# Two attention blocks on one core: V in loads of two octets, fewer remainder transposes by DMA, the first x in three parts, output in place

## The chip, the cores and the metric

The kernel runs on one core of a Trainium2 chip. The metric is the device time of one execution in microseconds; a time is the median of several runs, and one further execution was taken with the hardware profiler. [...]

## The reference

Two problems, A and B, with the same shapes and data of their own; their results stand side by side in the output.

```python
# per problem: x 16x80x576, k_cache and v_cache 16x16x512x128, wq 576x4096, wo 4096x576, all bf16
q = (x @ wq).reshape(B, Sq, 32, 128).transpose(0, 2, 1, 3)
k = jnp.repeat(k_cache, 2, axis=1)      # 16 KV heads serve 32 query heads
v = jnp.repeat(v_cache, 2, axis=1)
scores = jnp.einsum("bhqd,bhkd->bhqk", q, k) * (128 ** -0.5)
p = softmax(scores)
o = jnp.einsum("bhqk,bhkd->bhqd", p, v)
out = o.transpose(0, 2, 1, 3).reshape(B, Sq, 4096) @ wo
```

## The kernel before

**Steps.** An octet is four KV heads with their eight query heads. A step U takes one octet of one batch row; there are 128 steps, 64 for each problem. Octets go in pairs: an even step and the odd step after it take two neighbouring octets of the same batch row in turn, for the eight batch rows of one half of the batch. Each KV head of a step has two query heads of 80 rows, 160 rows. The first 128 of them make one tile of scores (512 keys wide); the last 32 of all four heads are packed into a fifth tile, the remainder. So a step has five tiles of 128x512: `qk` (L678) for four of them and `qkr` (L665) for the remainder.

**Path of a tile.** Scores in PSUM; the maximum on DVE (`em_max`, L687); the exponential on ACT with its row sum (`em_exp`, L691), which writes a slot of `p_sb`; the reciprocal on DVE (L697); the scaling on POOL (`em_nrm`, L700). TensorE then transposes P in 64x64 pieces (`em_tr`, L733), and DVE or ACT evicts it into `pT`: two evictions for the four main tiles (`ptev`, L751 and L752), two for the remainder (`prev`, L757 and L758). With `rtr` true the remainder of a step isn't transposed on TensorE: a DMA transpose (L740) on SP's queue takes it from `p_sb` into `pT`, and neither its eight transposes nor its two evictions are there. That holds for odd steps from `RT0` to `RT1`. `pv` (L781) multiplies with V, `oev` (L795) evicts to `oT`.

**Around the steps.** `qp` (L542) and its tail `qt` (L555) project x for later steps, `qev` (L568, L569) evicts Q. `op` (L827) multiplies a finished half of the heads with Wo in 20 pieces of 128x288 for each half of the heads. The first half's result goes into `acc` (L839, fp32); the second half's is added to it on DVE (`em_eb`, L856), written as bf16 into one of two buffers `osb` and stored (`em_st`, L862).

**Loads.** All go through SP's queue. K comes transposed by DMA, 1 MB for two steps, into one of three pairs of buffers (`em_ldk`, L631). V comes as 512 KB for each step into one of six buffers (`em_ldv`, L635). x of problem A comes in two parts for each half of the batch (L380); it lies in the memory of `acc`, which is free until the first output. TensorE transposes it (`xtr`, L401, and `xt`, L419). Wq comes in four pieces for the first two octets (L507, and L511 for its last 64 rows).

**Order.** Every operation belongs to a stream with a letter. The string `ORDER`, written out by hand, names the streams one after another; each letter takes the next operation of that stream, a quote mark puts it on the other of DVE and ACT, and digits give the PSUM banks. Each engine runs its operations in that order. `finalize` works out from reads and writes what an operation waits for; an engine that waits holds up everything behind it in its own order. Before the first transposes TensorE runs `NWARM` matmuls on zeros (L353).

## Time and profile before

| | us |
|---|---|
| median of 3 runs | 720.44 |
| lowest and highest | 718.01, 720.6 |
| profiled execution | 720.92 |
| its span, first to last instruction | 719.0 |

The granted TensorE clock was 1.0 in the profiled execution. Busy times are sums over instructions. The chain that ended last is followed back from the last instruction, at each step to what released it. "PE" is the matmuls, "PEld" the weight loads, which run beside them; "SPq" is SP's queue, and its entries are the issuing of DMAs. In the waits, a row names who waited, for whom, the microseconds in total, how many times, and the longest.

### The profile page before, as it was taken

To read this page: it belongs to the slowest core of one execution; us is meant where nothing else is said; L and a number is where in the kernel's file an instruction comes from. 1 tells how busy PE (TensorE), PEld (TensorE's weight loads), DVE (VectorE), ACT (ScalarE), POOL (GpSimd) and SP (SyncE) were. 2 spreads that over 40 slices of the span, in tenths; PEclk is the share of its full clock that TensorE was granted. 3 is DMA by queue.
4 is the path that set the end of the run, shared out by engine and by line. 5 is a ranking of instruction groups with operands and counts; after the bars stand their busy time and mean duration, and the time that the engine had idled before them with its cause. 6 is when DMAs were issued, how large, how long until landed. Compare 5 with 4: busy or idle time off the path is not lost.

```text
span 719.0 us, 25863 instructions
## 1 busy us (share of the span) xinstructions
PE 712.0 (99%) x10604; PEld 508.8 (71%) x10604; DVE 630.0 (88%) x1419; ACT 637.5 (89%) x1830; POOL 431.9 (60%) x650
## 2 busy tenths in 40 slices
PE   9999999999999999999999999999999999999998
PEld 5576777777777777777777776767677777777777
DVE  3999998899978998899998899878898889998995
ACT  1999998899988998799988999888999898998994
POOL 0467657566655765755774566645676466665783
PEclk9999999999999999999999999999999999999999
DMA  9999999999799998999999999999999999999970
GB/s 238 275 217 240 273 252 250 286 232 244 175 268 241 220 241 194 258 223 240 255 216 248 226 201 206 228 246 239 220 229 204 279 196 261 225 247 221 211 195 18
DMA packets 388853, 164.23 MB, mean 228 GB/s; under 512 B 293248, under 2 KB 385664, under 8 KB 388736
## 3 DMA queue, kind: packets, MB, share of 16 engines
q1 hardware_dynamic: 388736, 162.59, 100.2%
q8 instruction: 84, 1.38, 0.8%
q14 instruction: 33, 0.27, 0.2%
HBM read 87.65 MB, written 2.95 MB: 126 GB/s over the span
## 4 chain that ended last, share of the span: by engine, by line
PE 93%; DMA 2%; DVE 2%; ACT 1%; SPq 0%; issue 0%; ACTq 0%; DVEq 0%
PE ps L827 22%; PE ps L781 20%; PE ps L542 18%; PE ps L678 15%; PE ps L733 10%; PE ps L665 5%; PE ps L555 4%; DVE negmax L687 2%; DMA pT<-p_sb 1%; DMA wq_sb<-in_A_wq_dram 1%; DMA out_dram<-osb 1%; ACT p_sb L691 0%; ACT qT L568 0%; DVE xT L406 0%; DVE qT L569 0%
## 5 line engine op out<-in xcount | busy, mean ns | idle before, releaser
L700 POOL TENSOR_SCALAR p_sb<-p_sb,rinv 128x512 bf16<-128x512 bf16 x640 | 430.1, 692 | 271.4 <-DVE rinv L697 270.8
L691 ACT ACTIVATE p_sb<-ps,negmax 128x512 bf16<-128x512 f32 x640 | 442.7, 713 | 27.3 <-DVE negmax L687 23.5
L687 DVE TENSOR_REDUCE negmax<-ps 128x1 f32<-128x512 f32 x640 | 419.2, 682 | 35.0 <-PE ps L678 30.3
L781 PE MATMUL ps<-pT,v_sb 128*128 128x160 bf16 x2048 | 191.2, 233 | 1.1 <-ACT p_sb L691 0.8
L781 PEld LDWEIGHTS ps<-pT,v_sb 128*128 128x128 bf16 x2048 | 152.8, 98 | 42.6 <-ACT p_sb L691 4.1
L827 PE MATMUL ps<-wo_sb,oT 128*128 128x288 bf16 x1280 | 181.1, 286 | 0.0
L678 PE MATMUL ps<-kT,qT 128*128 128x512 bf16 x512 | 178.0, 380 | 1.2 <-ACT p_sb L691 0.8
L542 PE MATMUL ps<-xT,wq_sb 128*128 128x320 bf16 x1024 | 174.4, 299 | 0.2 <-DMA wq_sb<-in_A_wq_dram 0.2
L827 PEld LDWEIGHTS ps<-wo_sb,oT 128*128 128x128 bf16 x1280 | 122.0, 98 | 42.5 <-ACT p_sb L691 0.8
L691 ACT ACTIVATION_READ_ACCUMULATOR p_sb<-ps,negmax 128x1 f32 x640 | 146.0, 228 | 0.0
L542 PEld LDWEIGHTS ps<-xT,wq_sb 128*128 128x128 bf16 x1024 | 95.4, 98 | 45.0 <-ACT p_sb L691 2.4
L751 ACT COPY pT<-ps 128x512 f32<-128x512 f32 x157 | 92.4, 602 | 13.3 <-PE ps L733 12.8
L733 PEld LDWEIGHTS ps<-ident,p_sb 64*128 64x128 bf16 x4904 | 88.2, 95 | 7.3 <-issue 1.3
L733 PE MATMUL ps<-ident,p_sb 64*128 64x64 bf16 x4904 | 92.4, 190 | 0.3 <-issue 0.2
L752 DVE COPY pT<-ps 128x1024 bf16<-128x1024 bf16 x99 | 67.3, 684 | 11.4 <-PE ps L733 10.0
L568 ACT ACTIVATE qT<-ps 128x320 bf16<-128x320 f32 x133 | 59.0, 458 | 19.3 <-PE ps L555 15.5
L569 DVE TENSOR_SCALAR qT<-ps 128x320 bf16<-128x320 f32 x123 | 58.2, 482 | 10.7 <-PE ps L555 6.1
L795 DVE CAST oT<-ps 128x320 bf16<-128x320 f32 x122 | 58.4, 482 | 7.7 <-PE ps L781 7.4
L678 PEld LDWEIGHTS ps<-kT,qT 128*128 128x128 bf16 x512 | 48.0, 97 | 24.1 <-ACT p_sb L691 4.1
L795 ACT CAST oT<-ps 128x320 bf16<-128x320 f32 x134 | 58.9, 451 | 5.2 <-PE ps L781 4.9
L697 DVE RECIPROCAL rinv<-rowsum 128x3 f32<-128x3 f32 (+1 forms) x256 | 38.4, 160 | 1.8 <-ACT p_sb L691 1.7
L665 PE MATMUL ps<-kT,qT 128*32 128x512 bf16 x512 | 39.2, 384 | 0.0
(31 smaller groups left out, 175.5 us busy)
## 6 DMA issues: line engine op xcount, KB each, us to landing
v_sb<-in_A_v_cache_dram SPq DMA_DIRECT2D x64, 512.0 KB, 5.0
v_sb<-in_B_v_cache_dram SPq DMA_DIRECT2D x64, 512.0 KB, 5.2
wo_sb<-in_A_wo_dram SPq DMA_DIRECT2D x8, 576.0 KB, 5.8
wo_sb<-in_B_wo_dram SPq DMA_DIRECT2D x8, 576.0 KB, 5.8
wq_sb<-in_B_wq_dram SPq DMA_DIRECT2D x4, 1024.0 KB, 6.9
out_dram<-osb SPq DMA_DIRECT2D x40, 72.0 KB, 3.8
wq_sb<-in_A_wq_dram SPq DMA_DIRECT2D x8, 256.0 KB, 4.7
wq_sb<-in_A_wq_dram SPq DMA_DIRECT2D x2, 1024.0 KB, 8.4
```

The costliest lines, as they stand in the source:

```text
L542: last = e.matmul(ps[:, vbq[h].phys, QO:QO + 320], lhsT=wq_sb[:, wsl, ck, hi * 128:(hi + 1) * 128], rhs=xT[:, half, ck, n0:n0 + 320], star ...
L665: last = e.matmul(ps[32 * g4:32 * g4 + 32, vb_.phys, :], lhsT=qT[:, qsl_, bl_, g4 * 160 + 128:g4 * 160 + 160], rhs=k_of(U_, g4), start=Tru ...
L678: return e.matmul(ps[:, vb.phys, :], lhsT=qT[:, qsl, bl, gl * 160:gl * 160 + 128], rhs=k_of(U, gl), start=True, stop=True)
L687: return e.tensor_reduce(negmax[:, si:si + 1], ps[:, vb.phys, :], axis=AX.X, op=AluOpType.max, negate=True)
L691: return e.activation(p_sb[:, psl, :], ps[:, vb.phys, :], AF.Exp, bias=negmax[:, si:si + 1], scale=1.0, accum_out=rowsum[:, ss, k:k + 1])
L700: return e.tensor_scalar(p_sb[:, psl, :], p_sb[:, psl, :], rinv[:, ss, k:k + 1], 1.0, op0=AluOpType.mult, op1=AluOpType.mult)
L733: last = e.matmul(dst, lhsT=p_sb[64 * h:64 * h + 64, psls[k_], j * 128:(j + 1) * 128], rhs=ident[64 * h:64 * h + 64, 64 * h:64 * h + 64], ...
L751: return e.copy(dst.bitcast(F32), ps[:, vtp[h].phys, :].rearrange("p (j n) -> p j n", j=4))
L752: return e.tensor_copy(dst, psb[:, vtp[h].phys, :].rearrange("p (j n) -> p j n", j=4))
L781: last = e.matmul(ps[:, vo.phys, off:off + 160], lhsT=v_sb[:, vs, gl, j * 128:(j + 1) * 128], rhs=pT[:, pts, j, :, 32 * gl:32 * gl + 32], ...
L795: return (e.copy if en == "act" else e.tensor_copy)(dst, src)
L827: last = e.matmul(ps[:, vb.phys, 0:DC], lhsT=oT[:, sp_ * (HH // 2) + i, rb * 128:(rb + 1) * 128], rhs=wo_sb[:, 2 * c3 + sp_, i, :], start= ...
```

## The change

Four things, and an `ORDER` that is written anew throughout.

- **V** is loaded at even steps only, by one DMA of 1 MB for the step's own octet and the next one's, into a pair of neighbouring buffers; the load waits for both buffers. 64 loads instead of 128.
- **Remainder of P.** `RT0` goes from 71 to 97: the odd steps 71 to 95, thirteen of them, transpose their remainder on TensorE again and evict it; the odd steps 97 to 123, fourteen, keep the DMA.
- **First x.** x of the first half of the batch comes in three parts of one, two and two blocks of 128 rows instead of three and two. The one block is issued from ACT's queue, the others from SP's. `NWARM` goes from 8 to 5.
- **Output in place.** The last addition writes bf16 over the first half of the fp32 values that it reads in `acc`, and the store reads it there. `osb` is gone; an addition no longer waits for an earlier store.

On SP's queue the beginning changes from x (3 blocks), Wq 0, x (2 blocks), two of Wq's last rows, Wq 1, Wq 2 to x (2 blocks), Wq 0, two of Wq's last rows, x (2 blocks), Wq 1, Wq 2.

```diff
-NWARM = 8
+NWARM = 5
+VM = 1
...
-RT0 = 71
+RT0 = 97
...
-XLD = ((-100.0, -85.0), (-5.0, -4.9))
+XLD = ((-100.0, -99.9, -85.0), (-5.0, -4.9))
+XENG = (("act", "sp", "sp"), ("sp", "sp"))
...
-        XP = ((0, 3), (3, 5))
+        XPS = (((0, 1), (1, 3), (3, 5)), ((0, 3), (3, 5)))
...
-                S.add("sp", XLD[half][part], em_ldx,
+                S.add(XENG[half][part], XLD[half][part], em_ldx,
...
-            def em_ldv(e, vc_ap=vc_ap, b=b, q=q, vs=vs):
-                src = vc_ap[b, 4 * q:4 * q + 4, :, :].rearrange("g (p j) d -> p g (j d)", j=4)
-                return e.dma_start(v_sb[:, vs, :, :], src)
+            vw = 2 if VM else 1
+
+            def em_ldv(e, vc_ap=vc_ap, b=b, q=q, vs=vs, vw=vw):
+                src = vc_ap[b, 4 * q:4 * q + 4 * vw, :, :].rearrange("(w g) (p j) d -> p w g (j d)", w=vw, j=4)
+                return e.dma_start(v_sb[:, vs:vs + vw, :, :], src)
...
-            S.add("sp", 5.0 * U - VK, em_ldv, writes=[R(("V", vs), U)],
-                  dsem="d_v%d" % vs, name="ldv%d" % U, stream="V")
+            if U % vw == 0:
+                S.add("sp", 5.0 * U - VK, em_ldv, writes=[R(("V", (U + i_) % NV), U + i_) for i_ in range(vw)],
+                      dsem="d_v%d" % vs, name="ldv%d" % U, stream="V")
...
-                                return e.tensor_tensor(osb[:, slot, :], ps[:, vb.phys, 0:DC],
+                                return e.tensor_tensor(xs[:, rb, 2 * c3 * DC:(2 * c3 + 1) * DC], ps[:, vb.phys, 0:DC],
                                                        acc[:, rb, c3 * DC:(c3 + 1) * DC], AluOpType.add)
...
-                                return e.dma_start(dst, osb[:, slot, :])
+                                return e.dma_start(dst, xs[:, rb, 2 * c3 * DC:(2 * c3 + 1) * DC])
...
-                                  writes=[R(("osb", slot), (prob, half, n))], name="oeb%d.%d.%d" % (prob, half, n),
+                                  writes=[R(("acc", rb, c3), (prob, hh))], name="oeb%d.%d.%d" % (prob, half, n),
```

`xs` is the same memory as `acc`, read as bf16.

## The prediction

> **What bounds the kernel now.** I read the page of the profile first, then the busy time by stretches, then the chain in order of time, then the waits of single engines.

> ```profile
> span 719.0 us, 25863 instructions
> PE 712.0 (99%) x10604; PEld 508.8 (71%) x10604; DVE 630.0 (88%) x1419; ACT 637.5 (89%) x1830; POOL 431.9 (60%) x650
> ...
> PE 93%; DMA 2%; DVE 2%; ACT 1%; SPq 0%; issue 0%; ACTq 0%; DVEq 0%
> ```

> TensorE is busy 99% of the span and is 93% of the chain that ended last. A busy share alone could be an average over unlike stages, so the stretches come next (columns: length, then busy time and count of PE, PEld, DVE, ACT, POOL, then clock, DMA share, GB/s).

> ```profile
> 320.00:360.00 40.00, 40.00 (x649) 28.69 (x647) 39.52 (x93) 39.65 (x119) 26.58 (x41) 1.00 1.10 240
> ...
> 400.00:440.00 40.00, 39.84 (x580) 28.38 (x578) 36.32 (x82) 37.73 (x107) 26.04 (x39) 1.00 0.89 205
> 440.00:480.00 40.00, 39.76 (x581) 28.58 (x580) 34.50 (x77) 34.30 (x99) 23.73 (x37) 1.00 1.12 234
> 480.00:520.00 40.00, 38.73 (x563) 27.40 (x560) 33.11 (x72) 35.50 (x102) 23.81 (x36) 1.00 1.10 229
> 520.00:560.00 40.00, 40.00 (x609) 28.44 (x607) 36.14 (x81) 38.44 (x111) 26.58 (x40) 1.00 1.02 225
> ...
> 640.00:680.00 40.00, 39.91 (x614) 29.58 (x612) 35.59 (x78) 34.49 (x98) 25.23 (x38) 1.00 1.04 219
> 680.00:717.00 37.00, 36.40 (x566) 27.80 (x566) 29.60 (x69) 27.73 (x80) 21.81 (x33) 1.00 0.46 122
> ...
> 17.40:28.00 10.60, 10.24 (x77) 1.00 1.07 260
> 28.00:36.00 8.00, 7.59 (x108) 1.00 1.23 284
> ```

> From 320 to 360 us TensorE has no idle time at all, though DVE and ACT reach 39.5 and 39.7 of 40 us. What can be won is therefore small: its idle time from 400 to 520 us is 0.16 + 0.24 + 1.27 = 1.67 us, at the end 0.09 + 0.60 = 0.69 us, in the first steps 0.36 + 0.41 = 0.77 us. The rest is the head before the projections.

> **Remainder of P.** From step 71 to 95, thirteen odd steps lose their DMA transpose and get it back on TensorE.

> ```profile
> L740 SPq DMA_TRANSPOSE pT<-p_sb x27: 1188/1191/1850, 413.4 to 692.3; - x27
> ...
> 420.31 0.58 PE ps L733 x40
> ...
> 505.72 0.47 PE ps L733 x32
> ...
> 413.43 4.13 DMA pT<-p_sb
> ...
> 510.62 5.67 DMA pT<-p_sb
> ...
> ACT p_sb L691 <- DMA pT<-p_sb: 1.0, 2, 0.6
> ...
> PE ps L781 <- ACT p_sb L691: 0.8, 1, 0.8
> PE ps L678 <- ACT p_sb L691: 0.6, 2, 0.5
> ...
> PEld ps L781 <- ACT p_sb L691: 2.0, 3, 1.1
> PEld ps L678 <- ACT p_sb L691: 1.8, 4, 0.6
> ```

> The 27 DMA transposes stand 26 intervals of two steps apart, (692.3 − 413.4)/26 = 10.7 us, so a step is 5.36 us and the thirteen lie between 413 and about 550 us. A step with all transposes on TensorE has 40 in 0.58 us of the chain, one without the remainder 32 in 0.47 us: 0.11 us more each, 13 × 0.11 = 1.4 us, on the path, since nothing covers an instruction on a TensorE that never idles. In return the stalls of these steps go. The chain seems to offer 4.13 + 5.67 = 9.8 us for two DMA transposes, but a piece of the chain isn't a stall: an exponential that overwrites a remainder waited for the DMA that still read it, ACT lost 1.0 us by that, and TensorE waited 0.8 + 0.6 = 1.4 us for exponentials between 400 and 525 us. So the gain is at least this stretch's idle 1.67 us, at most what the weight loads waited there for exponentials, 2.0 + 1.8 = 3.8 us (gaps between records that modelled ends hide). I take 2.7, the middle. The chain's 9.8 is no end of the range, because TensorE worked during those pieces.

> The removed transposes also free the SP queue of 13 × 1.19 = 15 us, which I cost at nothing: that queue mostly waits (next part). New are 26 evictions of remainders:

> ```profile
> L757 ACT COPY pT<-ps 128x128 f32<-128x128 f32 x106 | 28.5, 284 | 7.6 <-PE ps L733 7.0
> L758 DVE COPY pT<-ps 128x256 bf16<-128x256 bf16 x96 | 26.1, 283 | 7.3 <-PE ps L733 6.5
> ```

> Counted in the written order, DVE gets 14 more (14 × 0.283 = 4.0 us) and ACT 12 (3.4 us), over 137 us: about 1.1 us in each 40. ACT's fullest stretch there, 38.44, becomes 39.5, which 320 to 360 us carries without TensorE idling. I take 0; without that cover it is 4.0 us.

> **V by pairs.** 64 loads of 1 MB take the place of 128 of 512 KB. The new load waits until both octets have been multiplied.

> ```profile
> v_sb<-in_A_v_cache_dram SPq DMA_DIRECT2D x64, 512.0 KB, 5.0
> ...
> wq_sb<-in_A_wq_dram SPq DMA_DIRECT2D x2, 1024.0 KB, 8.4
> ...
> L631 SPq DMA_TRANSPOSE kT<-in_A_k_cache_dram x32: 3971/5722/9905, 10.0 to 330.9; - x32
> ...
> DMA to landing us min/median/max: 6.1/8.4/13.4
> ...
> SPq L631 <- PE ps L678: 144.6, 21, 9.4
> ...
> SPq L635 <- PE ps L781: 17.4, 13, 6.4
> ```

> With six buffers, the load of steps U and U+1 may start after step U−5 instead of U−6: five steps ahead, 26.8 us, against 8.4 us for another load of 1 MB. V is not late. What is queued behind the waiting load is the next K transpose, the remaining DMA transposes of P, and weights. K needs three pairs of buffers, so it has two pairs of steps, 21.4 us, from free to used; less 8.4 us to landing that leaves 13 us. A V wait longer by a whole step (5.4 us) fits. I take 0, with −0.3 us on one side and a late K on the other (below). [...]

> **The head.** The first x comes as 144 KB from ACT's queue and two times 288 KB from SP's; five warm-up matmuls instead of eight.

> ```profile
> L507 SPq DMA_DIRECT2D wq_sb<-in_A_wq_dram x8: 477/508/605, 1.3 to 9.4; - x8
> ...
> DMA to landing us min/median/max: 3.9/4.7/5.6
> ...
> 3.79 4.45 DMA wq_sb<-in_A_wq_dram
> 8.37 2.33 PE ps L542 x16
> ...
> 1.24 3.60 PE L353 MATMUL ps<-wo_sb 128*128 128x512 bf16 x8 [1.24 <-DVE wo_sb L346]
> ...
> 4.48 1.37 PEld L401 LDWEIGHTS ps<-ident,acc 128*128 128x128 bf16 x12 [0.55 <-issue]
> ...
> 6.48 0.46 PEld L401 LDWEIGHTS ps<-ident,acc 128*128 128x128 bf16 x8 [0.31 <-DVE xT L406]
> ```

> The head ends when the second piece of Wq lands, 3.79 + 4.45 = 8.24 us. In the new order five loads still stand ahead of it on SP, with the same bytes in all, so I expect it there again; at best it takes the shortest landing, 3.9, a gain of 0.55. Earlier transposes of x are then only earlier idling, and four transposes (8 took 0.46 us) now stand behind that piece: +0.2 us. Three warm-ups less cost nothing by themselves: the eight ended at 4.84 and the first transpose came at 4.48. But the 12 transposes there took 0.114 us each, the 8 at 6.48 only 0.058, so TensorE doubled its rate after some 4.6 us of work; with five the warm-up ends at about 1.24 + 5/8 × 3.60 = 3.5 us, and a gap there may put that off. [...]

> **Output in place.** The addition that ends an output no longer waits until the store two before it has landed.

> ```profile
> 675.00 3.62 DMA out_dram<-osb
> ...
> PEld ps L733 <- DVE osb L856: 0.3, 1, 0.3
> ```

> Again the chain's 3.62 us is one wait that cost the weight loads 0.3 us. The gain lies between 0 and the end's whole idle 0.69; I take 0.4. New is that problem B's first write into a row of acc waits for A's store of it, which stands at least 28 steps earlier in the written order: 0. The last addition and store stay as they are.

> **The order itself** is rewritten. In steps 0 to 7 I count 19 evictions of Q on DVE before and 16 after, 9 of remainders before and 7 after, two of outputs more: 3 × 0.48 + 2 × 0.28 − 2 × 0.48 ≈ 1.0 us less on DVE where TensorE idles 0.77 us. I take −0.5, with ends −0.77 and +0.5 (an order could as well be worse by as much).

> **Sum.** +1.4 − 2.7 + 0 + 0.2 − 0.4 − 0.5 = −2.0 us. The profiled execution took 720.92 us (span 719.0 and 1.9 around it), so its like would take 718.9; the median of the three runs is 720.44, which gives **718.4 us**. The terms' own ends are 716.0 and 720.5.

> **Rivals.** *Every bubble goes.* Gains at their upper ends: −3.8 − 0.69 − 0.77 − 0.55 + 1.4 = −4.4, 716.0 us. For it: all these waits are named in the trace. Against it: new waits usually take the place of some. Chance 0.33.

> *K comes late behind V* (the other side). V's wait, up to 6.4 us now, is longer by a step, 11.8 us, with K behind it in the queue. That is still within 13 us; but a K transpose that lands in 13.4 us, the longest seen, has only 21.4 − 13.4 = 8.0 us to spare, and TensorE then stands for 3.8 us. Two such cases give 718.4 + 7.6 = 726.0 us. It decides from 13 us of wait, or 8 where DMA is crowded. Against it: SP already waits up to 9.4 us for K's own buffers, unharmed. Chance 0.14.

> *The evictions become the bound* between 413 and 550 us: 4.0 us more on DVE and 1.4 on TensorE without anything in return, less 0.9 at head and end: 724.9 us. It decides where ACT or DVE passes 40 of 40 us. Chance 0.10.

> [...] Chance 0.05.

> **How the numbers follow.** The forecast has 0.38, of which 0.05 lie below 716.8. A measurement here tells about 0.5% (3.6 us) from no change. Faster by more: 0.33 + 0.05 = 0.38; within: 0.33 + 0.05 = 0.38; slower: 0.14 + 0.10 = 0.24. The range reaches from below the first rival, 714.5 (an order that also packs the stretches after 560 us better), to the second, 726.0; the forecast's own is 716.0 to 720.5.

> **What would show it.** Right: 14 DMA transposes of P, 5008 transposes at L733, TensorE idle near 0.3 us in each 40 from 400 to 520 us; the second Wq piece still at 8.2 us; no wait for K or V. Wrong: TensorE waiting for kT or v_sb; DVE or ACT at 40 of 40 us with TensorE idle beside them; transposes still at 0.11 us after 8 us; Wq's second piece a microsecond earlier.

## The result and the profile after

| | before | after |
|---|---|---|
| median, us | 720.24 (718.01 to 720.6) | 723.53 (722.28 to 724.79) |
| profiled execution, us | 720.92 | 723.08 |
| its span, us | 719.0 | 721.4 |

The ratio after/before is 1.0051 with a 95% interval of 1.0031 to 1.0070: 3.3 us slower, where 718.4 us, 1.8 us faster than this median, was forecast. Four views answer to those of before; in all of them DVE is VectorE, ACT ScalarE, POOL GpSimd and SP SyncE. Behind the loads the line numbers of the changed kernel are three higher: PV is L784 instead of L781, the transposes of P are L736 instead of L733, the exponential L694 instead of L691. The page of the profile first:

```profile
span 721.4 us, 25960 instructions
...
PE 713.3 (99%) x10705; PEld 509.5 (71%) x10705; DVE 634.8 (88%) x1440; ACT 639.3 (89%) x1836; POOL 432.2 (60%) x651
...
PE 96%; ACT 2%; DMA 0%; issue 0%; DVE 0%; POOL 0%
```

TensorE has more of the chain (96% instead of 93%) and the DMA has left it: what the prediction saw in the chain did go. Yet the span is 2.4 us longer. The busy time by stretches, the kernel before first (from 40 us on, the stretches are 360, 120 and 197 us long), then after:

```profile
40.00:400.00 360.00, 360.00 (x5534) 258.96 (x5532) 326.09 (x741) 333.39 (x968) 221.66 (x330) 1.00 1.03 240
400.00:520.00 120.00, 118.33 (x1719) 84.35 (x1717) 103.93 (x230) 107.53 (x307) 73.57 (x110) 1.00 1.04 223
520.00:717.00 197.00, 196.05 (x2972) 143.42 (x2969) 173.15 (x386) 172.92 (x492) 123.31 (x184) 1.00 0.95 210
```

```profile
40.00:400.00 360.00, 358.47 (x5486) 257.13 (x5479) 325.14 (x736) 330.73 (x961) 221.74 (x330) 1.00 1.02 235
400.00:520.00 120.00, 120.00 (x1846) 86.78 (x1844) 106.23 (x243) 110.39 (x319) 73.94 (x111) 1.00 0.98 231
520.00:717.00 197.00, 196.39 (x3001) 143.50 (x2999) 177.10 (x402) 173.90 (x491) 124.37 (x185) 1.00 0.90 204
```

From 400 to 520 us TensorE's idle 1.67 us are gone, as forecast. From 40 to 400 us, where it had no idle time at all, it now has 1.53 us. No part of the change was expected to cost anything there. In the waits of TensorE the largest rows name no engine (the two last ones here belong to the head):

```profile
PE ps L668 <- issue: 0.9, 2, 0.6
PE ps L784 <- issue: 0.8, 2, 0.5
PE ps L736 <- issue: 0.6, 2, 0.3
PE ps L419 <- POOL acc L388: 0.6, 1, 0.6
PE ps L542 <- DVE xT L406: 0.5, 1, 0.5
```

"issue" says that the engine waited for nothing that the profile shows. No row is for kT or v_sb. The groups and DMA issues agree with what was counted: 5008 transposes, 14 DMA transposes of P, 64 loads of V.

```profile
L736 PE MATMUL ps<-ident,p_sb 64*128 64x64 bf16 x5008 | 94.1, 190 | 0.6 <-issue 0.6
```

```profile
v_sb<-in_A_v_cache_dram SPq DMA_DIRECT2D x32, 1024.0 KB, 6.4
v_sb<-in_B_v_cache_dram SPq DMA_DIRECT2D x32, 1024.0 KB, 6.3
...
pT<-p_sb SPq DMA_TRANSPOSE x14, 3.8
```

The head, in the timeline of TensorE (start, length, form, count):

```profile
1.24 2.31 PE L353 MATMUL ps<-wo_sb 128*128 128x512 bf16 x5 [1.24 <-DVE wo_sb L346]
4.14 0.29 PE L419 MATMUL ps<-ident,acc 128*128 128x128 bf16 x1 [0.59 <-POOL acc L388]
...
6.44 1.86 PE L542 MATMUL ps<-xT,wq_sb 128*128 128x320 bf16 x8 [0.52 <-DVE xT L406]
8.14 0.39 PE L401 MATMUL ps<-ident,acc 128*128 128x128 bf16 x4
8.37 1.25 PE L542 MATMUL ps<-xT,wq_sb 128*128 128x320 bf16 x8
```

The first 8 projections come half a microsecond earlier than before but take 1.86 us, the next 8 take 1.25: TensorE gets its full rate only some 1.3 us after they begin (the spacing of the projections falls from 0.267 to 0.136 us, and the trace has the full clock from 7.71 us on). The second piece of Wq is used at 8.37 us, as before, but for another reason: before, TensorE waited for it; here it has landed at 7.70 us, and TensorE comes to it late.

**An account of TensorE.** A busy sum hides short losses, so I also compare starts. Each kind of matmul has a spacing when nothing hinders it (scores 0.2147 us, projections 0.1365, PV 0.0692, Wo 0.1224, transposes of P 0.0144, and so on). Their sum, the warm-ups left out, is TensorE's work; the start of the last matmul less the work ahead of it is what it lost. Both kernels were profiled a second time (below), so each cell has both values, and the last column the difference of their means:

| us | before | after | difference |
|---|---|---|---|
| work | 688.12 | 689.62 | +1.50 |
| lost by 12 us | 5.90, 5.41 | 6.43, 7.53 | +1.32 |
| lost in pauses at multiples of 256 instructions (below) | 0.41, 1.96 | 2.98, 4.39 | +2.50 |
| lost elsewhere | 21.81, 19.89 | 19.59, 20.73 | −0.69 |
| last matmul starts | 716.12, 715.26 | 718.49, 722.14 | +4.63 |

In these profiled executions the kernels stand 4.6 us apart; the medians of the runs beside the second pair differ by 724.67 − 720.42 = 4.2 us, those of the first by 3.3. Two executions of each are few: the second one of after took 726.74 us, the longest of its six.

### The profile page after: what moved, and what is told of

The parts are those of the page before. It is cut to its first block, busy times and chain, and to the rows that moved or that the text cites. A ratio compares the mean times of both kernels' runs of the same rounds, so it can differ in the third digit from the quotient of the medians.

```text
span 721.4 us, 25960 instructions
## 1 busy us (share of the span) xinstructions
PE 713.3 (99%) x10705; PEld 509.5 (71%) x10705; DVE 634.8 (88%) x1440; ACT 639.3 (89%) x1836; POOL 432.2 (60%) x651
## 4 chain that ended last, share of the span: by engine, by line
PE 96%; ACT 2%; DMA 0%; issue 0%; DVE 0%; POOL 0%
PE ps L830 22%; PE ps L784 20%; PE ps L542 19%; PE ps L681 16%; PE ps L736 10%; PE ps L668 5%; PE ps L555 4%; ACT p_sb L694 2%; ACT qT L568 1%; DMA acc<-in_A_x_dram 0%; DVE xT L406 0%; PE ps L401 0%; ACT oT L798 0%; PE ps L456 0%; PE ps L419 0%
## 5 line engine op out<-in xcount | busy, mean ns | idle before, releaser
L694 ACT ACTIVATE p_sb<-ps,negmax 128x512 bf16<-128x512 f32 x640 | 442.7, 707 | 31.1 <-DVE negmax L690 26.5
L784 PE MATMUL ps<-pT,v_sb 128*128 128x160 bf16 x2048 | 190.7, 233 | 1.2 <-issue 0.8
L784 PEld LDWEIGHTS ps<-pT,v_sb 128*128 128x128 bf16 x2048 | 153.2, 98 | 40.3 <-issue 3.2
L542 PE MATMUL ps<-xT,wq_sb 128*128 128x320 bf16 x1024 | 174.1, 300 | 0.6 <-DVE xT L406 0.5
L694 ACT ACTIVATION_READ_ACCUMULATOR p_sb<-ps,negmax 128x1 f32 x640 | 142.0, 222 | 0.0
L542 PEld LDWEIGHTS ps<-xT,wq_sb 128*128 128x128 bf16 x1024 | 95.2, 98 | 47.0 <-issue 2.7
L754 ACT COPY pT<-ps 128x512 f32<-128x512 f32 x153 | 89.3, 599 | 11.6 <-PE ps L736 10.4
L736 PEld LDWEIGHTS ps<-ident,p_sb 64*128 64x128 bf16 x5008 | 89.8, 95 | 7.8 <-issue 1.5
L736 PE MATMUL ps<-ident,p_sb 64*128 64x64 bf16 x5008 | 94.1, 190 | 0.6 <-issue 0.6
L755 DVE COPY pT<-ps 128x1024 bf16<-128x1024 bf16 x103 | 70.1, 683 | 12.6 <-PE ps L736 11.4
L568 ACT ACTIVATE qT<-ps 128x320 bf16<-128x320 f32 x140 | 61.2, 456 | 17.3 <-PE ps L555 14.5
L798 DVE CAST oT<-ps 128x320 bf16<-128x320 f32 x127 | 60.6, 480 | 9.0 <-PE ps L784 8.5
L569 DVE TENSOR_SCALAR qT<-ps 128x320 bf16<-128x320 f32 x116 | 55.1, 481 | 9.7 <-PE ps L555 6.9
L798 ACT CAST oT<-ps 128x320 bf16<-128x320 f32 x129 | 56.9, 445 | 4.7 <-PE ps L784 4.1
## 6 DMA issues: line engine op xcount, KB each, us to landing
v_sb<-in_A_v_cache_dram SPq DMA_DIRECT2D x32, 1024.0 KB, 6.4
v_sb<-in_B_v_cache_dram SPq DMA_DIRECT2D x32, 1024.0 KB, 6.3
wq_sb<-in_B_wq_dram SPq DMA_DIRECT2D x4, 1024.0 KB, 6.4
wq_sb<-in_A_wq_dram SPq DMA_DIRECT2D x2, 1024.0 KB, 8.1
```

What stands on the lines that cost most here:

```text
L542: last = e.matmul(ps[:, vbq[h].phys, QO:QO + 320], lhsT=wq_sb[:, wsl, ck, hi * 128:(hi + 1) * 128], rhs=xT[:, half, ck, n0:n0 + 320], star ...
L694: return e.activation(p_sb[:, psl, :], ps[:, vb.phys, :], AF.Exp, bias=negmax[:, si:si + 1], scale=1.0, accum_out=rowsum[:, ss, k:k + 1])
L736: last = e.matmul(dst, lhsT=p_sb[64 * h:64 * h + 64, psls[k_], j * 128:(j + 1) * 128], rhs=ident[64 * h:64 * h + 64, 64 * h:64 * h + 64], ...
L754: return e.copy(dst.bitcast(F32), ps[:, vtp[h].phys, :].rearrange("p (j n) -> p j n", j=4))
L755: return e.tensor_copy(dst, psb[:, vtp[h].phys, :].rearrange("p (j n) -> p j n", j=4))
L784: last = e.matmul(ps[:, vo.phys, off:off + 160], lhsT=v_sb[:, vs, gl, j * 128:(j + 1) * 128], rhs=pT[:, pts, j, :, 32 * gl:32 * gl + 32], ...
```

## The experiments

Each time is a median, each ratio is to the kernel before on the same chip, with its 95% interval.

### Parts of the change alone, in the old order

The three parts that can be done without the new order were put into the old one, one by one and together. V by pairs, with each load at the odd step's place or 60 operations ahead of the first use, whichever is earlier:

```diff
+VM = 1
...
-            S.add("sp", 5.0 * U - VK, em_ldv, writes=[R(("V", vs), U)],
+            if U % vw == 0:
+                S.add("sp", 5.0 * U - VK, em_ldv, writes=[R(("V", (U + i_) % NV), U + i_) for i_ in range(vw)],
```

> The kernel before with V by pairs alone: 64 loads of 1 MB, each at the place that the odd step's load had in the written order, never less than 60 operations ahead of its first use. Theory 1 (the loss of 3.3 us comes from the newly written order and from TensorE's own extra work, not from the load's size): the time of before within 0.7 us. Theory 2 (the larger load delays what shares the DMA engines, TensorE's instruction fetches and the K transposes): 2 to 3 us slower, with more pauses of TensorE of 0.4 to 0.9 us in the middle of a group, where after has five (3.0 us in all) and before two (0.8 us).

Ten of the thirteen remainders back on TensorE (steps 85, 89 and 91 stay with the DMA, because the old order reuses their slots too early):

```diff
-RT0 = 71
+RT0 = 97
...
-            rtr = RT0 <= U < RT1 and (RTM[U % 2] or U >= RT2)
+            rtr = (RT0 <= U < RT1 or U in (85, 89, 91)) and (RTM[U % 2] or U >= RT2)
```

> The kernel before with ten of the thirteen remainders (steps 71 to 83, 87, 93, 95) transposed on TensorE again; 85, 89 and 91 stay with the DMA, because the old order reuses their slots too early. Theory 1 (the prediction's account of this part is right): TensorE gets 10 x 0.11 = 1.1 us more work and loses about 2 us less between 400 and 520 us, about 1 us faster. Rival (the stalls are the old order's, not the DMA's): they stay, 1.1 us slower.

Output in place, as in the change:

> The kernel before with its output written in place and no other change. The prediction's step: 0.4 us faster at the end. Rival (the wait for the store never held TensorE): the same time within 0.3 us.

All three:

> The kernel before with V by pairs, the ten remainders on TensorE and the output in place, in the old order. If the parts are innocent and the newly written order costs the time: 719 us, about 1 us under before. If the parts cost it: 722 to 724 us, as after.

Measured: V by pairs 727.56 us, 1.0104 (1.0090 to 1.0119); ten remainders 724.94, 1.0064 (1.0051 to 1.0076); in place 720.55, 1.0007 (0.9993 to 1.0022); all three 730.57, 1.0149 (1.0122 to 1.0177). The waits of TensorE with V by pairs:

```profile
PE ps L784 <- DMA v_sb<-in_A_v_cache_dram: 2.9, 1, 2.9
PE ps L784 <- DMA pT<-p_sb: 1.3, 2, 1.0
...
PE ps L784 <- ACT p_sb L694: 1.2, 1, 1.2
```

V came late once in the old order, by 2.9 of the roughly 7 us that this kernel is slower, and the ten remainders cost 4.7 us where the work is 1.15 us more. So the theory that every part is free by itself falls for these two. These runs say less of the change than they seem to: an operation put into an order that was written without it meets other waits than one that the order was written around. In place is a part with no such catch, and it does nothing that can be measured: the interval reaches from 0.5 us faster to 1.6 us slower.

### Parts undone in the new order

All 27 remainders by DMA again, each right behind its normalization and the last use of its buffer:

```diff
-RT0 = 97
+RT0 = 71
```

> The changed kernel with all 27 remainders by DMA again (RT0 = 71), each put behind its normalization. Theory of the prediction (in this stage the remainders on TensorE cost 1.4 us of work, and save 2.7 us of stalls between 400 and 520 us): work back to 688.1 us, the stalls of 0.3 to 1 us at the transposes back return between 400 and 520 us, and the time is 1 to 3 us over the changed kernel's. Rival (the stalls belonged to the old order; the new one leaves the DMA the time): the stalls stay away, and the time falls by the work, to 1 to 1.5 us under the changed kernel's.

V as two transfers of 512 KB at the place of the one:

```diff
-                return e.dma_start(v_sb[:, vs:vs + vw, :, :], src)
+                for i in range(vw):
+                    src = vc_ap[b, 4 * q + 4 * i:4 * q + 4 * i + 4, :, :].rearrange("g (p j) d -> p g (j d)", j=4)
+                    last = e.dma_start(v_sb[:, vs + i, :, :], src)
+                    if i < vw - 1:
+                        last.then_inc(sems["d_v%d" % vs], 16)
+                return last
```

> The changed kernel with V as two transfers of 512 KB, issued one behind the other at the place of the 1 MB transfer. Theory that the 1 MB transfer holds the queues (it stands ahead of the K transposes, whose ends the late instruction fetches follow): pauses and late fetches become fewer, 722 to 723. Rival (only the bytes and their place count): the same pauses at the same places, within 0.5 us of the changed kernel; SP needs 0.6 us more for each pair, which hides nothing and costs nothing as long as no K comes late.

With the DMA transposes 728.95 us, 1.0120 (1.0091 to 1.0149), some 5 us over the changed kernel. TensorE's stretch from 400 to 520 us, and its waits:

```profile
400.00:520.00 120.00, 115.50 (x1701) 82.15 (x1699) 99.84 (x222) 105.02 (x299) 71.46 (x107) 1.00 1.05 227
```

```profile
PE ps L784 <- DMA pT<-p_sb: 2.1, 2, 1.2
PE ps L830 <- ACT p_sb L694: 1.4, 1, 1.4
```

The stalls are back, and larger than before the change (4.5 us idle against 1.67). In this order the DMA transposes stall TensorE by more than the 1.5 us of work that they spare it. But how much of the 5 us is due to where I put them, this run can't tell, and the ten remainders in the old order went the other way: there it was slower with fewer DMA transposes. Either run moves operations within an order that was written without them, so the two don't show what a DMA transpose costs in its own order.

V in two transfers takes 723.49 us, 1.0045 (1.0028 to 1.0063): no different from the changed kernel. The size of V's transfer is worth nothing that can be measured here; that a load waits for two octets was not undone in the new order.

### The kernels again, and K by plain transfers

The pauses marked "issue" lie inside groups of like matmuls. My theory at this point: TensorE's next instructions are fetched too late. The profile lists a queue for that, here on the page of after (packets, MB, share):

```profile
q8 instruction: 84, 1.38, 0.8%
```

84 packets of 16 KB, one for every 259 or so of the 21,726 instructions of TensorE that the trace records. As the cause of a late fetch I took the K transposes, which hold SP's queue for 3.9 to 9.9 us each.

> The changed kernel unaltered, profiled a second time, to see which of its pauses come back. Instruction-fetch theory (TensorE pauses in the middle of a group because its next 256 instructions are fetched late): the pauses belong to places of the program where a fetch falls behind a long K transpose, so they recur at 62.9, 170.4, 178.5, 245.1 and 533.7 us within 1 us, some 2 to 3 us in all, and TensorE again loses 10 to 11 us beyond its work from 40 to 400 us. Chance theory (the pauses lie elsewhere in each execution and are as many in both kernels): other places, and the loss from 40 to 400 us may fall towards the 8.0 of the kernel before; then the 3.3 us need another cause. Time 722.5 to 724.5 either way.

> The kernel before unaltered, profiled a second time. Fetch theory: pauses near 474.7 and 624.9 us again and few elsewhere, under 1.5 us in all, loss from 40 to 400 us near 8.0. Chance theory: pauses at other places, 2 to 3 us in all as in the changed kernel. Time 719.5 to 721.

```diff
-                src = kc_ap[b, 4 * q:4 * q + 4 * w, :, :].rearrange("g (p j) d -> (g p) j d", j=4)
+                src = kc_ap[b, 4 * q:4 * q + 4 * w, :, :].rearrange("(w g) (p j) d -> p w g (j d)", w=w, j=4)
+                dst = kT[:, ks // 2, :].rearrange("p (w g n) -> p w g n", w=w, g=4)
...
-                return e.dma_start_transpose(dst, src)
+                return e.dma_start(dst, src)
```

> The changed kernel with K loaded by plain transfers of the same 1 MB in the same places instead of DMA transposes (K isn't transposed then). Fetch theory: SP no longer spends 4 to 9 us on each K, no fetch starts more than 330 instructions past its multiple of 256, the pauses in the middle of a group go, and with them 2 to 3 us: 719.5 to 721.5, and the distance to the kernel before with the same alteration falls to about 1 us (the 1.5 us more of TensorE work). Rival (the loss lies in the written order: TensorE reaches operands early): the pauses may go but the losses at waits stay, 722 to 724, still about 3 us above the other.

> The kernel before with K loaded by plain transfers of the same 1 MB in the same places (K isn't transposed then). Fetch theory: little to gain, 0.84 us of pauses, plus what P's DMA transposes gain by an SP queue that is free earlier (up to 3 us of the stalls from 400 to 520 us): 717 to 720. Rival (order): the same 717 to 720, but then 3 us or more under the changed kernel with the same alteration.

Measured: after again 724.67 us, 1.0060 (1.0036 to 1.0084); before again 720.42, 1.0000 (0.9982 to 1.0019). With plain K, after 722.09, 1.0025 (1.0010 to 1.0039), and before 719.29, 0.9980 (0.9962 to 0.9998).

The second profile of after has its pauses at the same instructions (64.5, 172.6 and 536.5 us for 63.0, 170.5 and 533.8, the whole being later by 1.5 to 3 us) and at two others. Before again has 3 pauses, 1.96 us in all, more than the 0.41 us of its first profile. So places recur, and whether a place shows a pause changes from one execution to the next. The stretch from 400 to 520 us isn't the same either, before again first, then after again:

```profile
400.00:520.00 120.00, 119.49 (x1770) 85.38 (x1767) 105.22 (x233) 109.10 (x312) 75.02 (x112) 1.00 1.02 225
```

```profile
400.00:520.00 120.00, 118.57 (x1795) 85.75 (x1794) 104.44 (x238) 108.99 (x315) 73.15 (x109) 1.00 0.98 229
```

Where the first pair of profiles had 1.67 us idle and then none, this pair has 0.51 and then 1.43, two pauses among them.

That K's transposes alone make the fetches late falls. With plain K, SP issues a K load in 0.37 us (the median in the changed kernel) instead of 3.9 to 9.9, and still both kernels have 6 fetches that begin over 330 instructions past their multiple of 256 (12 and 8 in the two profiles of after, 5 and 7 of before). The pauses remain, 2.2 us in the changed kernel. The distance between the two stays 2.8 us, where about 1 us was expected.

**What a pause is, exactly.** The trace gives each instruction of TensorE and each packet of the fetch queue a start. Counting from zero, fetch n normally begins when about 256n + 265 instructions are recorded (in the median 266 past the multiple of 256 in before's first profile, 268 in after's). The five pauses of after all fall where the count is 256n + 448, to the instruction. The twenty profiles of this study have 39 pauses of over 0.26 us at just that count, and of their pauses of 0.4 us or more between two matmuls of one kind all but two lie there (those two, 1.1 us with all remainders by DMA and 1.2 us with V by pairs in the old order, are waits between two operations). The view of the waits puts 7 of the 39 down to ACT; they lie at the same count, behind a fetch that began as late. I read that as the place by which fetch n must have taken effect; no record shows it directly. A normal fetch begins 183 instructions ahead of it. The fetch behind the pause had begun 337 to 437 past in 38 of the 39 cases (312 in the other), so 11 to 111 ahead, and 2.2 to 3.8 us before TensorE went on. The unhindered stream passes 111 instructions in 0.8 us where they are transposes of P (0.0144 us for a weight load and its matmul), in 3.8 us where they are PV's (0.0692). Two pauses in the timelines, of after and of the padded kernel below:

```profile
62.00 0.51 PE L784 MATMUL ps<-pT,v_sb 128*128 128x160 bf16 x5
63.01 0.94 PE L784 MATMUL ps<-pT,v_sb 128*128 128x160 bf16 x11 [0.50 <-issue]
```

```profile
41.48 0.30 PE L784 MATMUL ps<-pT,v_sb 128*128 128x160 bf16 x2
43.57 0.57 PE L784 MATMUL ps<-pT,v_sb 128*128 128x160 bf16 x6 [1.79 <-issue]
```

An operation at L784 is four matmuls, which wait for nothing once the first has begun; the one pause falls behind the fifth of 16 matmuls, so inside an operation, the other behind the second of eight. Most of the 84 or so fetches of an execution lead to no pause (79 of 84 in after's first profile), but those that do cost these kernels up to 4.7 us in one execution.

### The head

The changed kernel with the old head (x in two parts, both from SP, eight warm-ups; the first 87 operations of `ORDER` replaced by the old order's first 83, which do the same work):

```diff
-NWARM = 5
+NWARM = 8
...
-XENG = (("act", "sp", "sp"), ("sp", "sp"))
+XENG = (("sp", "sp"), ("sp", "sp"))
...
-        XPS = (((0, 1), (1, 3), (3, 5)), ((0, 3), (3, 5)))
+        XPS = (((0, 3), (3, 5)), ((0, 3), (3, 5)))
```

> The changed kernel with the head of the kernel before: first x in two parts, both from SP, eight warm-ups, and the first 83 operations in the old order; from there on the changed order. Cold-clock theory (in the changed head TensorE's first 8 projections, and in some executions the first 16, run at half speed, and the loss by 12 us is 6.3 to 8.2 us against 5.5 to 5.9): the first 24 projections take 0.14 us each, the loss by 12 us returns to 5.5 to 5.9, and the time falls by 0.4 to 2 us, to 721.8 to 723.5. Rival (the head is a wash: what it loses the ramp to 40 us takes up): 723 to 724.5.

The changed kernel with only the warm-ups back (`NWARM = 8`):

> The changed kernel with eight warm-ups of TensorE instead of five; x still in three parts. Cold-clock theory: full speed comes before the first projection, the 8 projections from 6.4 us take 1.15 us instead of 1.86 to 2.3, while the first x transposes wait some 0.9 us for the warm-ups to end; the loss by 12 us is 5.6 to 6.3 in every execution, and the time 722 to 723.5. Rival (the later transposes push the first projection back by as much): no change, 723 to 724.5.

The kernel before with the changed head, the same edit the other way round:

> The kernel before with the changed head: first x in three parts, the first of them from ScalarE's queue, five warm-ups, and the first 87 operations in the changed order; from there on the old order. Theory that the head costs by itself (slow clock at the first 8 to 16 projections, loss by 40 us 0.3 to 1.7 us up): 721 to 722.5. Theory that the head costs only through the pauses of the changed order that it brings about: the loss by 40 us is up by 0.3 to 0.9 us and the time by no more, 720 to 721.

Measured: old head in the changed kernel 721.62 us, 1.0021 (1.0005 to 1.0036); eight warm-ups 722.95, 1.0040 (1.0025 to 1.0055); changed head in the kernel before 722.08, 1.0025 (1.0008 to 1.0042). So the head costs some 2 us in either order. The timeline of the changed kernel's second profile shows a part of it:

```profile
6.40 2.31 PE L542 MATMUL ps<-xT,wq_sb 128*128 128x320 bf16 x8 [0.52 <-DVE xT L406]
8.51 0.63 PE L401 MATMUL ps<-ident,acc 128*128 128x128 bf16 x4
8.94 2.00 PE L542 MATMUL ps<-xT,wq_sb 128*128 128x320 bf16 x8
10.78 0.39 PE L401 MATMUL ps<-ident,acc 128*128 128x128 bf16 x4
```

and with the old head:

```profile
1.24 3.59 PE L353 MATMUL ps<-wo_sb 128*128 128x512 bf16 x8 [1.24 <-DVE wo_sb L346]
...
7.13 3.42 PE L542 MATMUL ps<-xT,wq_sb 128*128 128x320 bf16 x24
```

By the spacings of single matmuls (0.267 us for a slow projection, 0.136 for a fast one), the full rate came at about 7.8 us and 10.6 in the two profiles of the changed kernel and 9.5 in the kernel before with the changed head, after 5, 14 and 10 slow projections. Of the six profiles with five warm-ups and the changed head, one (all remainders by DMA) had it ahead of the first projection, the others at 7.8 to 10.6. With eight warm-ups it came between 4.2 and 6.9 us in nine profiles, always ahead of the first projection. The traces of seventeen of the twenty profiles also record when the full clock was granted; it is 6.44 us for before, 7.71 for after and 9.42 for the kernel before with the changed head; the last two agree with the spacings within 0.1 us. Each slow projection costs 0.13 us: 0.7 to 1.8 us. The loss by 12 us says the same: 6.4 to 7.5 us in the five profiles with the late rate, 5.8 in the one with the changed head and an early rate, 5.4 to 6.3 in the eight with the old head and eight warm-ups. That is about 1 us of the 2; where the rest of the head's cost lies isn't shown. The moment varies from one execution of a kernel to another, for the changed kernel by 2.8 us. What sets it isn't shown: between the warm-ups and the projections the changed head has transposes alone, but no run separates what they do.

Warm-ups alone bring the full rate back, and yet only 0.6 us of time, less than these intervals can tell:

```profile
6.95 1.26 PE L542 MATMUL ps<-xT,wq_sb 128*128 128x320 bf16 x8 [0.52 <-DVE xT L406]
...
11.82 1.25 PE L542 MATMUL ps<-xT,wq_sb 128*128 128x320 bf16 x8 [0.39 <-DMA wq_sb<-in_A_wq_dram]
```

The first projection comes 0.5 us later than with five (6.95 against 6.44), and then TensorE waits 0.4 us for a later piece of Wq, which lands at 11.68 us here and at 10.47 to 11.13 us in three profiles with the old head. By 12 us this kernel has lost some 6.6 us, no less than after. So the three warm-ups are no cure by themselves: in this head, what the clock gains is given back to a later start and to Wq. The profile of that kernel, the slowest of its eight executions, has 4.7 us of pauses at fetches besides.

### Shifting the fetches

If the pauses hang on where the multiples of 256 fall in the work, very small matmuls ahead of everything must move them (two instructions each, less two for each warm-up). They take the place of warm-ups:

```diff
+            for _ in range(NPAD):
+                last = e.matmul(ps[0:32, vw.phys, 0:32], lhsT=ones[:, 0:32], rhs=warm[:, 0, 0:32], start=True, stop=True)
```

Before, with `NPAD` 64 and 32 (`NWARM` 3 and 5):

> The kernel before with 64 very small matmuls for five of its eight warm-ups, each fetch 118 instructions earlier. Fetch theory: the kernel before had a lucky phase (8 us lost from 40 to 400 us), so here more pauses and 720.5 to 723. Rival: 719.5 to 720.8, pauses near 242 and 475 us as before.

> The kernel before with 32 very small matmuls for three of its eight warm-ups: every fetch 58 instructions earlier in the work. Fetch theory: late fetches at other places than with 0 or 118; the time lies anywhere from 719 to 724.5 and follows the sum of the pauses in the middle of a group in its profile (at 0: 0.8 us, at 118: 3 us or more). Rival (the 64 small matmuls cost by themselves, at the head): half of what they cost, 721.5 to 722.5, with the loss by 40 us up and not the pauses.

The changed kernel with the old head, `NPAD` 32, 64 and 96 (`NWARM` 5, 3 and 2):

> The changed kernel with the old head, in which three of the eight warm-ups are replaced by 32 very small matmuls: 64 instructions more and 6 fewer ahead of everything else, so each fetch falls 58 instructions earlier in the work. Fetch theory: the late fetches and the pauses move to other places, and the loss from 40 to 400 us may be anything from 8 to 12 us, with the time 720.5 to 724. Rival (the pauses hang on the work that is under way): the places stay (52 and 532 us), the loss stays at 8.8, and the time within 0.5 us of 721.6.

> As before with 64 very small matmuls for five warm-ups, so that each fetch falls 118 instructions earlier. Fetch theory: again other places, and a time that differs by 0.5 to 2 us from that with 32. Rival: 721 to 722.2, the same places.

> The changed kernel with the old head and 96 very small matmuls for six of its eight warm-ups: every fetch some 180 instructions earlier. Fetch theory: pauses at other places than with 0, 58 and 118; 719.5 to 723.5, by the sum of its pauses. To beat the kernel before (720.0), its loss would have to stay 1.5 us under that kernel's 28, as with 58 and 118 (25.5 and 26.4) and with fewer pauses still. Rival (the padding at the head does nothing that lasts): 721 to 721.8 as with 0 to 118.

| instructions ahead | before | changed, old head |
|---|---|---|
| 0 | 720.42; pauses 0.4, 2.0 | 721.62, 1.0021; 1.2 |
| some 60 | 723.28, 1.0040 (1.0027 to 1.0054); 0.0 | 720.88, 1.0014 (1.0002 to 1.0025); 0.5 |
| some 120 | 724.41, 1.0083 (1.0049 to 1.0118); 3.4 | 721.10, 1.0021 (1.0004 to 1.0037); 0.6 |
| some 180 | | 720.66, 1.0001 (0.9992 to 1.0009); 0.0 |

(Behind the semicolons the pauses of over 0.26 us at fetches in the profile, in us.) The row of the kernel before with 64 of them, for the stretch that had no idle time:

```profile
40.00:400.00 360.00, 357.00 (x5463) 256.76 (x5462) 323.35 (x736) 330.75 (x957) 221.42 (x330) 1.00 1.05 238
```

The old places are gone and there are others, with up to 1.96 us in one. That shows where they come from: the edit moves the count of instructions and swaps warm-ups in a head that loses no more (5.92 us by 12 us), and changes nothing behind it. The kernel before pays 4 us or more for 118 instructions. The new order is less touchy: all four of its versions lie within 1 us.

Two expectations were missed. With some 60 ahead, the kernel before is 2.9 us slower without any such pause in its profile (721.4 us, the fastest of its five runs); there it waits for exponentials:

```profile
PE ps L784 <- ACT p_sb L694: 2.4, 3, 1.1
```

So a shift acts on the old order in another way as well, which this profile doesn't settle. And no version is faster than the kernel before: with 180 ahead the changed one reaches 1.0001, some 3 us better than as it was written, and equal. So even with the old head and no pause in the profile the change brings none of the 2 us that were forecast.

## Why the prediction was wrong

The range (714.5 to 726.0) holds the 723.53 us; the forecast's own (716.0 to 720.5) doesn't, and the sign is wrong. By its steps:

- **Remainder transposes on TensorE, +1.4:** right, 1.50 by the account.
- **Stalls of the DMA transposes, −2.7:** right in kind. The idle time from 400 to 520 us went from 1.67 to 0.00; by the account that stretch lost 5.2, 3.5 and 4.1 us in three profiles with the old order, and 2.6 in after and in all four with the old head; after's second profile lost 4.1. But pauses at fetches lie in it, 0.4 and 0.7 us of the first two and 1.8 of the last. Without them it is 4.8, 2.8 and 4.1 us against 2.6 and 2.3: a gain of 0.2 to 2.5 us, 1.5 by the means. That pays for the 1.5 us of work and no more, where 1.3 us were to be left. The size was wrong: the idle 1.67 us was taken as the least that could be gained, and in the second profile of the same kernel it is 0.51.
- **Evictions, 0:** right. ACT's 110.39 and DVE's 106.23 us of 120 leave room, and TensorE doesn't idle there.
- **V by pairs, 0:** right for the new order (no wait for V or K; two half transfers take the same time). In the old order the same edit made V late: the 26.8 us of lead depended on the order.
- **Output in place, −0.4:** not seen; 1.0007 alone, with an interval that doesn't exclude 0.4 us.
- **The order, −0.5:** with the old head, the changed kernel loses 19.9 us outside head and pauses against 20.9 before, and that contains the stalls above. Of the gain that was expected in steps 0 to 7 little is there: from 12 to 40 us the profile before lost 2.80 us, after 2.61. And from 40 to 400 us the new order loses, pauses at fetches left out, 8.4 to 8.9 us in its ten profiles and the old one 7.4 to 8.1 in eight; what costs it that isn't known.
- **The gains together:** the first failed step, and the largest. Stalls, store and order were to bring 2.7 + 0.4 + 0.5 = 3.6 us; by the account all losses outside head and pauses fell by 0.7.
- **The head, +0.2:** the second failed step. It costs some 2 us in the runs, 1.3 by 12 us in the account. The prediction named a cause, that five warm-ups and a gap might put the doubled rate off, but it kept it out of the sum and gave it a chance of 0.05. None of its rows showed how late the rate could come; in the runs the late rate cost 0.7 to 1.8 us. Its own rows did speak for it: the eight warm-ups ended at 4.84 us and the rate doubled only after that (the trace has the full clock from 6.44 us on), so they showed no margin that five could be taken from. Calling them costless because the first transpose came at 4.48 weighed the wait and not the clock.
- **Nothing at all from 40 to 400 us:** the third failed step, and one that the text doesn't have. A stretch with no idle time and no edit but V was taken as one that can't get worse. It held a term that no edit was charged with: the places of the instruction fetches, which move with every instruction added ahead. Here that was some 2.5 us against the change in these two pairs of profiles. With the other kernels that keep each order's count (before with the output in place and with plain K, 2.0 and 1.2 us of pauses; after with V in two transfers and with plain K, 2.4 and 2.3) it is about 1.7. Whether the kernel before stood at a good place stays open: of its padded versions one has 3.4 us of pauses and one none.

Work +1.5, head +1.3 by 12 us, pauses +2.5 and all other losses −0.7 make the 4.6 us between the profiled executions. From the forecast −2.0 that is 6.6 us: 2.9 of them are gains that did not come, 2.5 pauses, 1.1 the head and 0.1 work. Of the rivals, the late full rate in the head, the one with a chance of 0.05, came true, though beside gains that did not come, and so with a longer time; K late and full evictions did not occur.

What stays open: why a fetch begins late. In the eighteen profiles with K transposes, of 157 that began over 330 past 64% did so between 1 us before and 2 us after SP was done with a K transpose, where about 44% of all fetches lie: these transposes may add to it, but taking them away didn't end it. Why the old order slows at 60 instructions without a pause. What the new order loses more from 40 to 400 us. And where the part of the head's 2 us lies that isn't there by 12 us.

## What to carry to other kernels

Where TensorE is busy 99% of the span, a difference of half a per cent can come from where the instruction fetches fall (here pauses of 0.0 to 4.7 us in an execution of some 720): look at the pauses marked "issue" in the middle of a group, for a pause under another name count the instructions ahead of it, and repeat a comparison with some tens of small instructions ahead before an edit is blamed or praised. Warm-up matmuls are to be counted to the moment at which the rate doubles, with the spread between executions (here 4.2 to 6.9 us with eight; 7.7 to 10.6 with five and the changed head, but for one profile), and not to the first moment at which there is other work; but they also put off what stands behind them (here the first projection by 0.5 us), so both are weighed. A stall is sized from more than one profile: the stretch from which this forecast took 2.7 us was idle for 1.67 us in one execution and for 0.51 in the next. A part tried alone in an order written for something else measures the fit as much as the part.
